# Mixer GEMMs run class by class beside attention of the other class, with buffers that live for the whole kernel

## The chip, the cores and the metric

The kernel runs on one core of a Trainium2 chip. The metric is the device time of one execution in microseconds (us); the kernel before takes 1502.11 us (median of 3 runs, 1501.19 to 1504.04).

PE is the matmul engine (PEld its weight load), DVE the vector engine, ACT the scalar engine, POOL the GpSimd engine, SP the engine that issues DMAs. PSUM is the memory that PE writes to. Each engine has its own queue of instructions, whose order is fixed when the program is built; each keeps to that order, even where a later instruction is ready.

## The reference, cut to what matters

```python
# S = 2048 tokens, D = 1024, 32 heads of 32, window W = 8 with dilation 2, F = 3584
def A(x):                       # sliding local attention
    q, k, v = split_heads(x @ wqkv)
    # token s looks at tokens s, s-2, ..., s-14: all of its own parity
    logits = einsum("bhsd,bhswd->bhsw", q, k[window(s)]) * DH ** -0.5
    o = einsum("bhsw,bhswd->bhsd", softmax(mask(logits)), v[window(s)])
    return merge_heads(o) @ wo
def B(x):                       # token-mixing MLP, contracts over ALL tokens
    h = layernorm(x)
    u = gelu(einsum("bsd,sf->bdf", h, w1) + b1)          # GEMM1
    return (einsum("bdf,fs->bds", u, w2) + b2).transpose # GEMM2
x = A_x
for layer in (1, 2):
    x = x + A(layernorm(x))
    x = x + B(layernorm(x))
```

Attention never mixes even and odd tokens, because the dilation is 2. The kernels call each parity a *class* and work on one class, split into 4 groups of 8 heads, at a time: 8 *chunks* in a layer. GEMM1 sums over all tokens, so it can be split by class into two partial sums. GEMM2 gives each token's output by itself, so it can be split by class too.

## The kernel before

Scores and weighted sums are elementwise work on DVE. Q, k, v and the output projection are matmuls.

```python
def qk(ci):                                        # scores of one chunk
    for w in range(W):
        pr = t4p.tile([P, J, QW], BF16, tag="t4")  # 3 buffers
        mult(pr, q_sb, k_window(w))                # 128x2048
        add(pr, halves of pr)                      # 128x1024
        add(St[:, w], quarters of pr)              # 128x512
    ...                                            # softmax
def pv(ci):                                        # weighted sum of v
    if c == 0: ... 8 x (DVE multiply, 4 matmuls with the identity add up in PSUM)
    else:      ... 8 DVE multiplies, 7 DVE adds
# ... after the chunks, for the first class:
for j in range(J):                                 # out-projection + residual; statistics on ACT
    ...
    nc.scalar.activation(out=junk2, in_=xn, func=ACT.Square, bias=nm[:, j], accum_out=ss[:, j])
nc.gpsimd.tensor_scalar(out=sc, in0=ss, scalar1=(1.0 + EPS) / D, scalar2=EPS * EPS, ...)   # L331
nc.gpsimd.tensor_tensor(out=sc, in0=sc, in1=mhalf, op=ALU.pow)
nc.gpsimd.tensor_tensor(out=bi, in0=nm, in1=sc, op=ALU.mult)                               # L334
for j in range(J):
    nc.scalar.activation(out=h2[0][..j..], in_=xq, func=ACT.Identity, bias=bi[:, j], scale=sc[:, j])
# GEMM1 partial sums of the first class (5 of 7 blocks of F), then layer_B:
# the rest of GEMM1, then GEMM2 for all tokens, then layernorm and transposes for the next layer
```

The layers run one after the other: attention, GEMM1, all of GEMM2, attention again. In the trace the first class's out-projection (L301, 228 to 301 us) and part of its GEMM1 partial sums already run beside the second class's chunks, although the program text has them after the chunks.

Of the kernel before, what the change touches and what calls it, by code (L numbers as in the profile page):

```python
# [1 line left out]

# [11 lines left out]
P = 128  # L14
# [9 lines left out]

@with_exitstack
def kernel(
# [11 lines left out]
):  # L38
    nc = tc.nc
# [11 lines left out]
    NT = S // P  # L51
    JH = J // 2
    assert D == H * DH and R == 16 and J == 8 and W - 1 <= J and QW == 256 and D % 512 == 0 and KD == 2 * NQ
    NDC = D // 512
    FB = 512
    NFB = F // FB
    SBW = 256
    scale = float(DH) ** -0.5
    NPART = 5
    GF = FB // P  # L60

    const = ctx.enter_context(tc.tile_pool(name="const", bufs=1))
    stat = ctx.enter_context(tc.tile_pool(name="stat", bufs=4))
    x2p = ctx.enter_context(tc.tile_pool(name="x2p", bufs=4))
    jkp = ctx.enter_context(tc.tile_pool(name="jkp", bufs=1))
    hxp = ctx.enter_context(tc.tile_pool(name="hxp", bufs=4))
    dram = ctx.enter_context(tc.tile_pool(name="dram", bufs=1, space=bass.MemoryType.DRAM))
    w1ep = ctx.enter_context(tc.tile_pool(name="w1ep", bufs=2))
    gpp = ctx.enter_context(tc.tile_pool(name="gpp", bufs=1))
    psmm = ctx.enter_context(tc.tile_pool(name="psmm", bufs=2, space=bass.MemoryType.PSUM))  # L70
    pstp = ctx.enter_context(tc.tile_pool(name="pstp", bufs=2, space=bass.MemoryType.PSUM))
    psop = ctx.enter_context(tc.tile_pool(name="psop", bufs=2, space=bass.MemoryType.PSUM))
    psgp = ctx.enter_context(tc.tile_pool(name="psgp", bufs=2, space=bass.MemoryType.PSUM))
    rr = [0]

    def ps_any():
        rr[0] += 1
        pool, tag = ((psmm, "ps"), (psop, "pso"), (psgp, "psg"))[rr[0] % 3]
        return pool.tile([P, 512], FP32, name=tag, tag=tag)

    def x2(name):
        return x2p.tile([P, D], BF16, name=name, tag="x2")
# [3 lines left out]

    ident = const.tile([P, P], BF16, name="ident")
    make_identity(nc, ident[:])
    maskq = const.tile([P, W, J, HQ], FP32, name="maskq")
    nc.vector.memset(maskq[:], 0.0)  # L90
    for w in range(1, W):
        nc.vector.memset(maskq[0:1, w, 0:w, :], NEG)
    mhalf = const.tile([P, R], FP32, name="mhalf")
    nc.vector.memset(mhalf[:], -0.5)
    b1_bf = const.tile([P, FT], BF16, name="b1_bf")
    b2_bf = const.tile([P, NT], BF16, name="b2_bf")
    with nc.allow_non_contiguous_dma(reason="tiny bias loads"):
        nc.sync.dma_start(out=b1_bf[:], in_=B_b1.rearrange("(t p) -> p t", p=P))
        nc.sync.dma_start(out=b2_bf[:], in_=B_b2.rearrange("(t p) -> p t", p=P))
    b1_sb = const.tile([P, FT], FP32, name="b1_sb")  # L100
    b2_sb = const.tile([P, NT], FP32, name="b2_sb")
    nc.vector.tensor_copy(out=b1_sb[:], in_=b1_bf[:])
    nc.vector.tensor_copy(out=b2_sb[:], in_=b2_bf[:])

    xs_a1 = dram.tile([S, D], BF16, name="xs_a1")
    xs_b1 = dram.tile([S, D], BF16, name="xs_b1")
    xs_a2 = dram.tile([S, D], BF16, name="xs_a2")

    def halo_view(t2d):
        return t2d.rearrange("(p r) d -> p r d", r=R)  # L110

    def ln_single_dve(x_ap, out_ap):
        nch = D // 512
        st = stat.tile([P, nch, 6], FP32, name="ln_st", tag="ln_st")
        for c in range(nch):
            nc.vector.bn_stats(out=st[:, c, :], in_=x_ap[:, c * 512:(c + 1) * 512])
        mv = stat.tile([P, 2], FP32, name="ln_mv", tag="ln_mv")
        nc.vector.bn_aggr(out=mv[:], in_=st[:])
        ve = stat.tile([P, 1], FP32, name="ln_ve", tag="ln_ve")
        nc.gpsimd.tensor_scalar(out=ve[:], in0=mv[:, 1:2], scalar1=EPS, scalar2=None, op0=ALU.add)  # L120
        rstd = stat.tile([P, 1], FP32, name="ln_rstd", tag="ln_rstd")
        nc.gpsimd.tensor_tensor(out=rstd[:], in0=ve[:], in1=mhalf[:, 0:1], op=ALU.pow)
        nb = stat.tile([P, 1], FP32, name="ln_nb", tag="ln_nb")
        nc.gpsimd.tensor_tensor(out=nb[:], in0=mv[:, 0:1], in1=rstd[:], op=ALU.mult)
        nc.gpsimd.tensor_scalar(out=nb[:], in0=nb[:], scalar1=-1.0, scalar2=None, op0=ALU.mult)  # L125
        nc.scalar.activation(out=out_ap, in_=x_ap, func=ACT.Identity, bias=nb[:], scale=rstd[:])  # L126

    def transposes(h_ap, tp):
        for kt in range(KD):
            nc.tensor.transpose(tp[:, kt, :], h_ap[:, kt * P:(kt + 1) * P], ident[:])  # L130

    def new_hT():
        return [[hx(f"hT{c}{jh}", [P, KD, JH, P]) for jh in range(2)] for c in range(DIL)]

    def layer_A(li, hT, res_src, xs_dst, prologue=None):
        res_v = halo_view(res_src)
        dst_v = halo_view(xs_dst)
        wq_v = A_wqkv.rearrange("(kt p) c -> p kt c", p=P)
        wo_v = A_wo.rearrange("(qi hl b a) n -> qi b a hl n", qi=NQ, hl=HQ, b=2, a=16)
        h2 = [[None, None], [None, None]]  # L140
        A = ExitStack()
        wqp = A.enter_context(tc.tile_pool(name=f"wqp{li}", bufs=3))
        qp = A.enter_context(tc.tile_pool(name=f"qp{li}", bufs=2))
        kvp = A.enter_context(tc.tile_pool(name=f"kvp{li}", bufs=1))
        stp = A.enter_context(tc.tile_pool(name=f"stp{li}", bufs=1))
        t4p = A.enter_context(tc.tile_pool(name=f"t4p{li}", bufs=3))
        oqp = A.enter_context(tc.tile_pool(name=f"oqp{li}", bufs=1))
        otp = A.enter_context(tc.tile_pool(name=f"otp{li}", bufs=5))
        wop = A.enter_context(tc.tile_pool(name=f"wop{li}", bufs=1))
        smp = A.enter_context(tc.tile_pool(name=f"smp{li}", bufs=1))  # L150
        if prologue is not None:
            hT = prologue()
        oT_all = [[None] * NQ for c in range(DIL)]
        chunks = [(c, qi) for c in range(DIL) for qi in range(NQ)]
        st8 = {}

        def proj(ci, parts_):
            c, qi = chunks[ci]
            d = st8.setdefault(ci, {})
            for part in parts_:  # L160
                wt = wqp.tile([P, KD, QW], BF16, name=f"w{part}", tag="wq")
                nc.sync.dma_start(out=wt[:], in_=wq_v[:, :, part * D + qi * QW: part * D + (qi + 1) * QW])
                if part == 0:
                    buf = qp.tile([P, J, QW], BF16, name="q_sb", tag="q_sb")
                    d["q"] = buf
                else:
                    buf = kvp.tile([P, NSLOT, QW], BF16, name="k_sb" if part == 1 else "v_sb", tag="k_sb" if part == 1 else "v_sb")
                    d["k" if part == 1 else "v"] = buf
                    nc.gpsimd.memset(buf[0:1, 0:W - 1, :], 0.0)  # L169
                for jp in range(J // 2):  # L170
                    ps = psmm.tile([P, 2, QW], FP32, name="ps", tag="ps")
                    for jj in range(2):
                        j = 2 * jp + jj
                        for kt in range(KD):
                            nc.tensor.matmul(ps[:, jj, :], lhsT=hT[c][j // JH][:, kt, j % JH, :], rhs=wt[:, kt, :],  # L175
                                             start=(kt == 0), stop=(kt == KD - 1))
                    if part == 0:
                        dst = buf[:, 2 * jp:2 * jp + 2, :]
                    else:
                        dst = buf[:, W - 1 + 2 * jp:W + 1 + 2 * jp, :]  # L180
                    nc.scalar.activation(out=dst.rearrange("p j (d h) -> p j d h", h=HQ),  # L181
                                         in_=ps[:].rearrange("p j (h d) -> p j d h", d=DH), func=ACT.Identity)
                if part > 0:
                    nc.sync.dma_start(out=buf[1:113, 0:W - 1, :], in_=buf[0:112, W:NSLOT, :])
                    nc.sync.dma_start(out=buf[113:128, 0:W - 1, :], in_=buf[112:127, W:NSLOT, :])

        def qk(ci):
            q_sb, k_sb = st8[ci]["q"], st8[ci]["k"]
            St = stp.tile([P, W, J, DH // 4, HQ], BF16, name="St", tag="St")
            for w in range(W):  # L190
# [30 lines left out]

        def pv(ci):
            c, qi = chunks[ci]
            v_sb, Pb = st8[ci]["v"], st8[ci]["P"]
            o_q = oqp.tile([P, J, QW], BF16, name="o_q", tag="o_q")
            ov = o_q[:].rearrange("p j (d h) -> p j d h", h=HQ)
            on_pe = (c == 0)
# [280 lines left out]
```

## Time and profile before

| stretch, us | what | PE busy | DVE busy |
|---|---|---|---|
| 0 to 54 | prologue (layernorm of x, first projections) | 25.5 | 29.6 |
| 54 to 388 | attention, layer 1 | 276.2 | 292.5 |
| 388 to 775.5 | out-projection of the second class, GEMM1, GEMM2 | 380.9 | 109.9 |
| 775.5 to 1128 | attention, layer 2 | 294.5 | 293.1 |
| 1128 to 1502.5 | out-projection, GEMM1, GEMM2 | 370.6 | 72.0 |

Two answers of the profile stand behind it. First, the page of the kernel before: busy time and share of the span, then the span in 40 slices, where a digit is the busy share in tenths (PEclk: the granted matmul clock in tenths).

```profile
PE 1347.7 (90%) x7968; PEld 764.5 (51%) x7968; DVE 797.1 (53%) x1155; ACT 432.6 (29%) x692; POOL 145.8 (10%) x180
...
PE   3599999929999999999987998997399999999998
...
DVE  5799999973703202323217999999465231011111
...
PEclk9899999969999999999998999999699999999999
```

Second, the busy table by stretches. The columns after the stretch are its length, then busy us (and instructions) of PE, PEld, DVE, ACT and POOL, the granted clock, the DMA share and GB/s.

```profile
0.00:54.00 54.00, 25.53 (x237) 21.98 (x238) 29.62 (x70) 20.27 (x21) 8.53 (x16) 0.94 0.88 248
54.00:388.00 334.00, 276.21 (x2024) 191.98 (x2022) 292.52 (x396) 127.55 (x226) 48.14 (x17) 0.93 0.30 91
388.00:568.00 180.00, 179.82 (x834) 81.39 (x833) 50.49 (x80) 61.30 (x84) 9.35 (x32) 1.00 0.36 108
568.00:775.50 207.50, 201.04 (x1024) 94.91 (x1022) 59.37 (x110) 32.02 (x48) 22.29 (x66) 0.99 0.36 106
775.50:1128.00 352.50, 294.50 (x2141) 206.60 (x2142) 293.13 (x396) 130.13 (x232) 48.49 (x19) 0.93 0.28 84
1128.00:1502.50 374.50, 370.57 (x1717) 167.67 (x1714) 71.98 (x107) 61.38 (x83) 8.98 (x31) 1.00 0.31 94
```

How to read this: in the GEMM stretches DVE has little to do and PE is full. In the attention stretches DVE is the fuller engine. Matmuls are pipelined and their ends modelled, so "PE busy" overstates work: a 128x512 matmul is shown with 379 ns but starts every 216 ns. Counted with 216 and 109 ns (128x256), PE has about 1312 us of work, so about 190 us of the span are idle PE or a low clock.

The dip is worth a closer look, as the timeline shows it (start, duration, engine, line, operation, and in brackets the idle time before and what ended it). These lines are from the POOL, ACT, PE and DVE timelines of the kernel before.

```profile
18.54 0.27 POOL L458 TENSOR_SCALAR r_197<-mvall 128x8 f32<-128x8 f32 x1 [14.22 <-DVE mvall L456]
...
305.34 24.20 POOL L331 TENSOR_SCALAR sc<-ss 128x8 f32<-128x8 f32 x1 [14.72 <-ACT junk L328]
...
331.60 4.63 ACT L339 ACTIVATE h_3236<-xq,bi,sc 128x1024 bf16<-128x1024 bf16 x4 [26.35 <-POOL bi L334]
...
332.89 4.41 PE L351 MATMUL psg<-h_3236,w1e 128*128 128x512 bf16 x8 [28.40 <-ACT h_3236 L339]
...
328.27 1.21 DVE L254 TENSOR_TENSOR o_q<-o_q,pvtmp 128x2048 bf16<-128x2048 bf16 x1
350.11 0.42 DVE L214 TENSOR_TENSOR m_3058<-L 128x256 f32<-128x256 f32 x1 [20.63 <-ACT L L208]
```

One POOL instruction on 128x8 elements takes 24.20 us; one of the same shape (an add alone, not a multiply and an add) took 0.27 us in the prologue, where DVE was idle. It ends at 329.54, when DVE ends its last operation (328.27 + 1.21 = 329.48). ACT waits for POOL, PE for ACT, and DVE for an Exp (L208) that stands in ACT's order behind the work that waits for POOL.

### The profile page before, as it was taken

The page shows a single profiled execution, that of the slowest core. Times are in us where ns is not written, and L with a number is a line of the kernel's source. Part 1 is how long each engine was busy: PE and PEld are TensorE (multiplying, and loading weights), DVE is VectorE, ACT ScalarE, POOL GpSimd, SP SyncE. Part 2 cuts the span into 40 slices and gives each one's busy share as a digit, 9 for nine tenths or more (in the row PEclk, how much of TensorE's full clock was granted, in tenths as well). Part 3 has the DMA queues.
Part 4 walks back from the last instruction along what each step waited for, and adds up shares of the span by engine and source line. Part 5 has one row for each costly group of instructions (what it writes and reads, how often), then busy time and mean ns, then how long its engine had stood idle before and what let it go on. Part 6 is the DMA issues. An engine that isn't in the chain of part 4 may idle for free.

```text
span 1502.5 us, 19132 instructions
## 1 busy us (share of the span) xinstructions
PE 1347.7 (90%) x7968; PEld 764.5 (51%) x7968; DVE 797.1 (53%) x1155; ACT 432.6 (29%) x692; POOL 145.8 (10%) x180
## 2 busy tenths in 40 slices
PE   3599999929999999999987998997399999999998
PEld 3576776604444444444456676764144444444444
DVE  5799999973703202323217999999465231011111
ACT  3323434424344321111122333355343442100000
POOL 1001000070200000000010001002502000000000
PEclk9899999969999999999998999999699999999999
DMA  8632223314392205343312322233146321034340
GB/s 231 209 93 67 85 75 110 96 59 128 105 252 73 68 28 147 92 140 92 91 43 68 91 69 81 84 99 109 35 132 200 115 73 47 1 94 137 114 126 34
DMA packets 177655, 150.04 MB, mean 100 GB/s; under 512 B 11712, under 2 KB 150976, under 8 KB 177568
## 3 DMA queue, kind: packets, MB, share of 16 engines
q1 hardware_dynamic: 177568, 148.82, 33.3%
q8 instruction: 62, 1.02, 0.3%
q14 instruction: 25, 0.20, 0.0%
HBM read 117.45 MB, written 16.78 MB: 89 GB/s over the span
## 4 chain that ended last, share of the span: by engine, by line
PE 57%; DVE 29%; POOL 4%; ACT 3%; issue 3%; DMA 3%; SPq 0%; DVEq 0%; POOLq 0%; ACTq 0%
PE pso L426 9%; PE psg L426 8%; PE ps L426 8%; DVE pr L192 8%; DVE pvtmp L232 6%; PE psg L386 6%; PE ps L386 6%; PE psg L351 5%; PE pso L386 5%; PE ps L175 5%; DVE pr L194 4%; PE pso L301 3%; POOL sc L331 3%; DVE o_q L254 3%; DVE St L195 2%
## 5 line engine op out<-in xcount | busy, mean ns | idle before, releaser
L192 DVE TENSOR_TENSOR pr<-q_sb,k_sb 128x2048 bf16<-128x2048 bf16 x128 | 153.6, 1213 | 22.4 <-ACT k_sb L181 18.1
L232 DVE TENSOR_TENSOR pvtmp<-v_sb,Pb 128x2048 bf16<-128x2048 bf16 x120 | 142.7, 1217 | 15.1 <-DMA v_sb<-v_sb 12.7
L386 PEld LDWEIGHTS <-w1o 128*128 128x128 bf16 x896 | 87.6, 98 | 105.8
L351 PEld LDWEIGHTS <-w1e 128*128 128x128 bf16 x640 | 63.1, 99 | 143.5 <-issue 72.7
L429 DVE SCALAR_TENSOR_TENSOR xo<-pso,b_sb,xs 128x512 bf16<-128x512 f32 x22 | 16.5, 751 | 160.7 <-PE pso L426 150.3
L429 DVE SCALAR_TENSOR_TENSOR xo<-ps,b_sb,xs 128x512 bf16<-128x512 f32 x21 | 15.8, 751 | 156.8 <-PE ps L426 146.0
L194 DVE TENSOR_TENSOR pr<-pr 128x1024 bf16<-128x1024 bf16 x128 | 85.7, 683 | 0.1
L181 ACT ACTIVATE k_sb<-ps 128x512 bf16<-128x512 f32 x64 | 36.7, 596 | 120.7 <-DVE pr L192 63.9
L351 PE MATMUL psg<-h_3236,w1e 128*128 128x512 bf16 x160 | 44.2, 395 | 29.4 <-ACT h_3236 L339 28.4
L351 PE MATMUL psg<-h_9265,w1e 128*128 128x512 bf16 x160 | 43.2, 388 | 29.4 <-ACT h_9265 L339 28.4
L429 DVE SCALAR_TENSOR_TENSOR xo<-psg,b_sb,xs 128x512 bf16<-128x512 f32 x21 | 15.8, 751 | 101.4 <-PE psg L426 90.9
L254 DVE TENSOR_TENSOR o_q<-o_q,pvtmp 128x2048 bf16<-128x2048 bf16 x56 | 68.1, 1215 | 0.1
L243 PE MATMUL pva<-pvtmp,ident 128*128 128x512 bf16 x256 | 63.8, 378 | 4.5 <-DVE pvtmp L232 1.2
L181 ACT ACTIVATE v_sb<-ps 128x512 bf16<-128x512 f32 x64 | 36.6, 595 | 72.5 <-DVE pvtmp L232 38.1
L181 ACT ACTIVATE q_sb<-ps 128x512 bf16<-128x512 f32 x64 | 38.2, 599 | 58.6 <-PE ps L175 58.6
L126 ACT ACTIVATE hb<-xo,ln_nb,ln_rstd 128x1024 bf16<-128x1024 bf16 x16 | 19.8, 1240 | 119.5 <-POOL ln_nb L125 119.5
L130 PE MATMUL tph<-ident,hb 128*128 128x128 bf16 x256 | 22.6, 240 | 35.0 <-ACT hb L468 28.9
L169 POOL MEMSET k_sb<- 1x1792 bf16 x16 | 25.3, 1582 | 283.1 <-DVE pr L192 258.1
L175 PEld LDWEIGHTS <-hT_4990 128*128 128x128 bf16 x384 | 40.0, 104 | 23.3 <-issue 15.8
L195 DVE TENSOR_TENSOR St<-pr 128x512 bf16<-128x512 bf16 x128 | 51.4, 415 | 0.1
L331 POOL TENSOR_SCALAR sc<-ss 128x8 f32<-128x8 f32 x2 | 48.4, 24202 | 29.4 <-ACT junk L328 29.4
L175 PEld LDWEIGHTS <-hT_145 128*128 128x128 bf16 x384 | 38.5, 101 | 20.7 <-issue 14.8
(993 smaller groups left out, 2624.5 us busy)
## 6 DMA issues: line engine op xcount, KB each, us to landing
w1e<-in_B_w_dram SPq DMA_DIRECT2D x14, 1024.0 KB, 5.4
w1o<-in_B_w_dram SPq DMA_DIRECT2D x14, 1024.0 KB, 5.4
xt<-in_A_x_dram SPq DMA_DIRECT2D x32, 256.0 KB, 3.9
k_sb<-k_sb SPq DMA_DIRECT2D x16, 392.0 KB, 4.8
v_sb<-v_sb SPq DMA_DIRECT2D x16, 392.0 KB, 4.8
xr<-in_A_x_dram SPq DMA_DIRECT2D x16, 256.0 KB, 2.8
xs_a_114<-xn SPq DMA_DIRECT2D x16, 256.0 KB, 2.0
xs<-xs_a_114 SPq DMA_DIRECT2D x16, 256.0 KB, 2.9
```

The source lines that it names most:

```text
L175: nc.tensor.matmul(ps[:, jj, :], lhsT=hT[c][j // JH][:, kt, j % JH, :], rhs=wt[:, kt, :], start=(kt == 0), stop=(kt == KD - 1))
L181: nc.scalar.activation(out=dst.rearrange("p j (d h) -> p j d h", h=HQ), in_=ps[:].rearrange("p j (h d) -> p j d h", d=DH), func=ACT.Identity)
L192: nc.vector.tensor_tensor(out=pr[:], in0=q_sb[:], in1=k_sb[:, W - 1 - w:W - 1 - w + J, :], op=ALU.mult)
L194: nc.vector.tensor_tensor(out=pv[:, :, 0:16, :], in0=pv[:, :, 0:16, :], in1=pv[:, :, 16:32, :], op=ALU.add)
L195: nc.vector.tensor_tensor(out=St[:, w], in0=pv[:, :, 0:8, :], in1=pv[:, :, 8:16, :], op=ALU.add)
L232: nc.vector.tensor_tensor(out=dst, in0=vw, in1=pw, op=ALU.mult)
L243: nc.tensor.matmul(accs[g][:], lhsT=ident[:], rhs=tf[:, g * 512:(g + 1) * 512], start=(w == 0), stop=(w == W - 1))
L254: nc.vector.tensor_tensor(out=ov, in0=ov, in1=tv, op=ALU.add)
L331: nc.gpsimd.tensor_scalar(out=sc[:], in0=ss[:], scalar1=(1.0 + EPS) / D, scalar2=EPS * EPS, op0=ALU.mult, op1=ALU.add)
L351: nc.tensor.matmul(ps[:], lhsT=w1e[:, j, fl * P:(fl + 1) * P], rhs=h2[0][j // JH][:, j % JH, dc * 512:(dc + 1) * 512], start=(j == 0), sto ...
L386: nc.tensor.matmul(ps[:], lhsT=w1b[c][:, j, fl * P:(fl + 1) * P], rhs=h2[c][j // JH][:, j % JH, dc * 512:(dc + 1) * 512], start=(k == 0), ...
L426: nc.tensor.matmul(ps[:], lhsT=w2b[ft // HF][:, ft % HF, tl * P:(tl + 1) * P], rhs=g[ft // GF][:, ft % GF, dc * 512:(dc + 1) * 512], start ...
```

## The change

The intent is to keep PE full in attention, with GEMM work of the other class.

- GEMM2 is done class by class. After layer 1, the first class's GEMM2 runs, and layer 2's attention starts on that class at once; the second class's GEMM2 is woven into it. The first class's out-projection and GEMM1 partials are woven into the second class's attention, now in an order made by hand.
- All buffers live for the whole kernel, so nothing waits for a pool to close between layers. The three work buffers of scores and sums become one, T4, of two windows. The transposes of the attention output share one PSUM bank, where they had two in turn.
- DVE operations of the scores, and of the sums made on DVE, cover two windows each (128x4096). In layer 2 no weighted sum is made on PE.
- The scale of the layernorms comes from Ln and Exp on ACT, not from POOL.
- For the first layernorm x is read once, into the space of GEMM1's output, not twice; the residual still reads it again.

The core of the diff; cuts are marked with `...`.

```diff
-    for w in range(W):
-        pr = t4p.tile([P, J, QW], BF16, name="pr", tag="t4")
-        nc.vector.tensor_tensor(out=pr[:], in0=q_sb[:], in1=k_sb[:, ...], op=ALU.mult)
-        ... add halves, add quarters into St[:, w]
+    for u0 in range(0, W, WB):                       # WB = 2, one buffer T4
+        nc.vector.tensor_tensor(out=flat, in0=qb, in1=windows(k, u0, WB, ...), op=ALU.mult)
+        ... add halves, quarters, eighths into St[:, u0:u0 + WB]
+        yield 0.0, 4.9                               # (PE us, DVE us) for the weave
...
-    nc.gpsimd.tensor_scalar(out=sc[:], in0=ss[:], ...)
-    nc.gpsimd.tensor_tensor(out=sc[:], in0=sc[:], in1=mhalf[:, 0:J], op=ALU.pow)
+    nc.scalar.activation(out=ln[:], in_=var, func=ACT.Ln, bias=eps[:], scale=mul)
+    nc.scalar.activation(out=dst, in_=ln[:], func=ACT.Exp, scale=-0.5)
...
+    for b in range(2):                               # transposes of the attention output
+        tp = pstp.tile([P, J, P], BF16, name="tpo", tag="tpa")      # one PSUM bank
+        ... 8 transposes; nc.scalar.copy(out=oT[:, b], in_=tp)
...
+    # GEMM2 of one class: every second column of w2 is the weight
+    nc.tensor.matmul(ps[:], lhsT=w2t[ft // HF][:, ft % HF, c::DIL], rhs=g[...], ...)
...
+    def weave(lead, fill, then, last):
+        for unit in chain(lead, last):
+            if unit == "second":                     # the other class must be ready: drain
+                for u in fill: add(u)
+                ...
+            if unit == "out":                        # let out-projection and partials in
+                fill, then = then or fill, None
+                ...
+            add(unit)
+            while t[0] < t[1]: add(next(fill))       # give PE as much as DVE has got
...
+    weave(at_.stream(), second_class(),
+          chain(out_proj(at_, 0, ..., on_act=True), partials()),
+          out_proj(at_, 1, ..., on_act=False))
+    ... rest of GEMM1; layer 1: GEMM2 of the first class; layer 2: GEMM2 of both
```

The function `weave` works while the program is built. Each unit of attention, and each unit of the GEMM work that is to fill its gaps (the fill), comes with the author's estimate of its PE and DVE time. `weave` adds these up in two accounts, and while PE's account is below DVE's, it issues fill.

## The prediction

> **What bounds the kernel now.** The busy table by stretches splits the 1502.5 us in two. The dense stretches, 388 to 762 and 1128 to 1502 us (out-projection of the second class, GEMM1, GEMM2), are full of matmuls: the chain of waits shows 128x512 matmuls every 0.216 us (28 in 6.04 us) and 128x256 ones every 0.109 us (32 in 3.50 us). The other 754 us are attention and what leads into it. There VectorE (DVE) leads: 204.9 us PE and 217.3 us DVE busy in the 220 us from 80 to 300; then PE is busy for 10 of 40 us (300 to 340, granted clock 0.62), in the chain behind a 24.2 us POOL instruction (pow) of the layernorm. The prologue delays dense PE work to about 80 us; 762 to 775 is a gap.
>
> PE work at those rates (an estimate): 2 x (1536 x 0.109 + 2048 x 0.216) = 1220, weighted sum of v on PE 256 x 0.216 = 55, residuals 7, transposes about 30: 1312 us. So PE idles, or waits on a low clock, some 190 us.
>
> **What the change does.**
> - Removes 128 weighted-sum matmuls (layer 2 sums on DVE): PE falls to about 1284 us; DVE gains 28 adds of 1.215 us, 34 us.
> - Removes POOL pow (2 x 24 us in the chain) for Ln and Exp on ACT.
> - Loads x once and early; first-class layernorm on DVE. First score multiply at about 38 us instead of 54, without the 32 us that the first chunk's scores took.
> - Layer 1: no second-class GEMM2 (97 us) before attention; it fills layer 2's attention. Out-projection (31 us) and GEMM1 partials (69 us) of the first class fill the second class's chunks.
> - DVE ops get twice as wide but run in dependent order on one T4 buffer: dependent ops start their duration plus 0.04 us apart, independent ones 0.08 us under it. Two windows of scores: about 4.75 us against 4.2 before plus the share of one 2048-wide add. I see little DVE gain: about 35 us per chunk with sums on PE, 43.5 with sums on DVE.
>
> **Sum (estimates from those durations).** Layer 1: scores start 38; 4x35 + 4x43.5, plus 10 us of DVE waiting for PE in the weighted sums: 362. Out-projection 28 + 5: 395. GEMM1 rest 576 x 0.216: 519. First-class GEMM2 and transposes: 620. Layer 2: layernorm latency, k and q of chunk 0: 641. Four chunks 174 + 12 of GEMM2 evictions + 5: 832. Second-class projection cannot start before its GEMM2 ends, so DVE idles about 22: 854. Four chunks + 5: 1033. Out-projection 32: 1065. GEMM1 608 x 0.216: 1196. GEMM2 193.5 + 3: about 1392.
>
> The strided weight load (every second column of w2) should stay hidden: a load takes 98 ns against 216, and the Trainium skill, "TensorE: Matmul & The Clock Gate", section on weight-path modes, allows fast weight load with column steps up to 1,024 elements. No run here shows it yet.
>
> **Predicted 1390 us**, 8 in 10 within 1345 to 1440. Faster by over 2%: 0.96; within 2%: 0.03; slower: 0.01.
>
> **What would show it.** Right: no POOL work in the chain; first score multiply near 38; dense stretches at 0.216 us; attention about 325 us in layer 1 and 395 in layer 2, DVE over 90% busy there; a DVE hole near 20 us where layer 2 changes class; 100 to 120 us of PE idle left.
>
> **What would make it wrong.** w2 loads (1.8 MB per 12 us, six buffers) stalling first-class GEMM2; weight loads above 216 ns; in-order DVE stalling on woven evictions (slower); the wide DVE ops losing or gaining rate; less idle at the joints than I charge (faster, toward 1340).

## More of the kernel before

The two dips of PE to 2 and 3 in the slices fall into the attention stretches, at about 300 and 1050 us.

## The result

The changed kernel takes 1398.7 us (median of 4 runs, 1396.64 to 1400.82), the kernel before 1502.88 us in the same rounds. The ratio is 0.9305 (95% interval 0.9289 to 0.9321). A ratio is the mean time of one kernel's fast runs over that of the other's of the same rounds, so it is not quite the ratio of the medians quoted. Run again, the changed kernel took 1399.62 us (ratio 0.9308).

> The changed kernel once more, so that the other runs of this call can be compared with it on the same chip. Both theories: 1395 to 1402 us.

The page of the changed kernel, the same lines as before:

```profile
PE 1314.1 (94%) x7840; PEld 749.7 (54%) x7840; DVE 818.0 (59%) x928; ACT 483.4 (35%) x940; POOL 10.5 (1%) x20
...
PE   6999989999899999999899989899949999999998
...
DVE  4869999999820433327999939929976023211111
...
PEclk9999999999999999999999999999969999999999
```

PE's 128 fewer instructions are the weighted sums moved to DVE in layer 2. POOL's work inside the layers is gone (10.5 us are left, in the first slice). One dip of PE is left, about slice 30 (1010 to 1050 us). DVE has dips to 3 and 2 inside layer 2's attention that were not there before. The busy table by stretches of the changed kernel, with bounds at its own events:

```profile
0.00:358.50 358.50, 323.53 (x2369) 222.58 (x2370) 311.19 (x336) 193.87 (x399) 10.49 (x20) 0.99 0.40 114
358.50:615.50 257.00, 255.88 (x1226) 117.06 (x1227) 86.02 (x140) 55.99 (x97) 0.00 (x0) 0.99 0.43 127
615.50:634.50 19.00, 18.84 (x161) 15.09 (x160) 2.85 (x5) 5.86 (x11) 0.00 (x0) 1.00 0.46 138
634.50:817.00 182.50, 173.06 (x1178) 111.24 (x1177) 174.23 (x172) 75.52 (x150) 0.00 (x0) 0.98 0.50 145
817.00:839.60 22.60, 19.52 (x168) 15.48 (x167) 0.34 (x2) 12.05 (x22) 0.00 (x0) 1.00 0.44 128
839.60:1037.00 197.40, 169.72 (x1124) 109.03 (x1123) 165.18 (x156) 91.92 (x183) 0.00 (x0) 0.94 0.34 95
1037.00:1394.90 357.90, 353.54 (x1625) 159.25 (x1623) 78.17 (x120) 48.24 (x78) 0.00 (x0) 0.99 0.34 102
```

Against the kernel before, by bounds that mark nearly the same events: layer 1's attention ends at 358.5 in place of 388 (29.5 us earlier; by the start of its last transposes, 358.5 against 382.8, it is 24). The GEMM stretch of layer 1 is 257 us in place of 387.5: half of GEMM2 (97 us) is gone from it, and 576 GEMM1 matmuls are left after the last transposes of attention in place of 727 (counted by their weight loads; 151 x 0.216 is 33 us). Layer 2, from its first projections to the end of attention (615.5 to 1037), takes 421.5 in place of 352.5 us, because that half is now in it. The last stretch is 357.9 in place of 374.5, as 608 GEMM1 matmuls are left after attention in place of 727. The sum, -29.5 - 130.5 + 69 - 16.6, is -107.6, the difference of the two profiled spans.

DVE's timeline of the changed kernel shows its two big holes in layer 2. The first operation of both attentions is here as well.

```profile
39.46 2.29 DVE L288 TENSOR_TENSOR T_126<-q_116,k_118 128x4096 bf16<-128x4096 bf16 x1 [16.24 <-DMA k_118<-k_118]
...
634.51 2.29 DVE L288 TENSOR_TENSOR T_126<-q_116,k_118 128x4096 bf16<-128x4096 bf16 x1 [14.16 <-ACT q_116 L275]
...
839.58 2.29 DVE L288 TENSOR_TENSOR T_126<-q_116,k_118 128x4096 bf16<-128x4096 bf16 x1 [22.26 <-ACT q_116 L275]
...
941.99 1.22 DVE L346 TENSOR_TENSOR o_q<-T_126 128x2048 bf16<-128x2048 bf16 x1 [23.78 <-PE tpo L357]
```

The hole of 22.26 us is the class change: the second class's projections cannot begin before its GEMM2, layernorm and transposes are done. The one of 23.78 us was not foreseen. DVE wants to write o_q, but PE has not yet transposed the previous chunk's o_q. The PE and ACT timelines say why:

```profile
892.88 1.06 PE L357 MATMUL tpo<-ident,o_q 128*128 128x128 bf16 x8
...
940.30 0.99 ACT L358 COPY oT<-tpo 128x1024 bf16<-128x1024 bf16 x1
...
941.34 0.61 PE L357 MATMUL tpo<-ident,o_q 128*128 128x128 bf16 x8
```

The first half was transposed at 892.88. Its copy out of the one PSUM bank stands in ACT's order behind the layernorm of woven out-projection tiles and runs at 940.30, 47 us later; in between ACT idles for 1.25 us several times while it waits for an out-projection tile. Only then can PE transpose the second half and release o_q. PE itself was busy meanwhile with the woven work, but then idles 17.7 us before the last transposes:

```profile
1034.35 1.03 PE L357 MATMUL tpo<-ident,o_q 128*128 128x128 bf16 x8 [17.70 <-DVE o_q L350]
```

### The profile page after: what moved, and what is told of

It reads as the page before. It is cut to its first block, busy times and chain, and to the rows that moved or that the text cites. A ratio compares the mean times of both kernels' runs of the same rounds, so it can differ in the third digit from the quotient of the medians.

```text
span 1394.9 us, 18742 instructions
## 1 busy us (share of the span) xinstructions
PE 1314.1 (94%) x7840; PEld 749.7 (54%) x7840; DVE 818.0 (59%) x928; ACT 483.4 (35%) x940; POOL 10.5 (1%) x20
## 4 chain that ended last, share of the span: by engine, by line
PE 56%; DVE 35%; ACT 6%; issue 2%; DMA 2%; SPq 0%; DVEq 0%; ACTq 0%
PE psg L488 11%; PE pso L488 9%; PE psg L466 9%; DVE T_126 L321 8%; PE ps L273 7%; DVE T_126 L288 7%; PE pso L433 6%; PE pso L466 5%; PE ps L466 4%; DVE T_126 L289 4%; DVE o_q L350 3%; DVE T_126 L349 3%; DVE T_126 L290 2%; DVE St L291 1%; DVE xo L493 1%
## 5 line engine op out<-in xcount | busy, mean ns | idle before, releaser
L433 PE MATMUL pso<-wo,oT 128*128 128x512 bf16 x512 | 121.5, 389 | 0.7 <-DVE xn L439 0.4
L288 DVE TENSOR_TENSOR T_126<-q_116,k_118 128x4096 bf16<-128x4096 bf16 x32 | 73.2, 2289 | 55.5 <-ACT q_116 L275 36.4
L433 PEld LDWEIGHTS <-oT 128*128 128x128 bf16 x512 | 50.4, 100 | 62.2 <-issue 7.5
L321 DVE TENSOR_TENSOR T_126<-v_120,Pb 128x4096 bf16<-128x4096 bf16 (+1 forms) x40 | 74.0, 1864 | 11.7 <-PE psg L336 10.8
L289 DVE TENSOR_TENSOR T_126<-T_126 128x2048 bf16<-128x2048 bf16 x64 | 78.1, 1221 | 1.2
L288 DVE TENSOR_TENSOR T_126<-q_117,k_119 128x4096 bf16<-128x4096 bf16 x32 | 73.1, 2284 | 4.1 <-PE psg L336 2.2
L321 DVE TENSOR_TENSOR T_126<-v_121,Pb 128x4096 bf16<-128x4096 bf16 (+1 forms) x40 | 73.8, 1864 | 0.9
L273 PE MATMUL ps<-wq,hT_152 128*128 128x256 bf16 x384 | 51.4, 288 | 4.7 <-DMA wq<-in_A_wqkv_dram 2.1
L273 PE MATMUL ps<-wq,hT_6303 128*128 128x256 bf16 x384 | 46.5, 280 | 4.6 <-ACT v_120 L275 4.2
L273 PE MATMUL ps<-wq,hT_4874 128*128 128x256 bf16 x384 | 46.5, 280 | 4.5 <-ACT v_120 L275 4.1
L358 ACT COPY oT<-tpo 128x1024 bf16<-128x1024 bf16 x32 | 32.3, 1010 | 47.3 <-PE tpo L357 47.3
L273 PE MATMUL ps<-wq,hT_153 128*128 128x256 bf16 x384 | 44.9, 273 | 3.1 <-ACT hT_153 L244 2.5
L273 PEld LDWEIGHTS <-hT_152 128*128 128x128 bf16 x384 | 38.9, 103 | 14.3 <-ACT hT_152 L244 2.9
L273 PE MATMUL ps<-wq,hT_810 128*128 128x256 bf16 x384 | 44.9, 273 | 1.7 <-ACT q_117 L275 1.0
L273 PE MATMUL ps<-wq,hT_811 128*128 128x256 bf16 x384 | 45.5, 273 | 0.4 <-ACT v_120 L275 0.4
L290 DVE TENSOR_TENSOR T_126<-T_126 128x1024 bf16<-128x1024 bf16 x64 | 44.0, 688 | 1.4
L350 DVE TENSOR_TENSOR o_q<-o_q,T_126 128x2048 bf16<-128x2048 bf16 x36 | 44.1, 1225 | 1.2
L349 DVE TENSOR_TENSOR T_126<-T_126 128x2048 bf16<-128x2048 bf16 x36 | 44.1, 1224 | 1.1
```

Source lines behind the costliest of these rows:

```text
L273: nc.tensor.matmul(ps[:, jj, :], lhsT=self.hT[c][j // JH][:, kt, j % JH, :], rhs=wts[part][:, kt, :], start=(kt == 0), stop=(kt == KD - 1))
L288: nc.vector.tensor_tensor(out=flat, in0=qb, in1=windows(k, u0, WB, [(1, J * QW)]), op=ALU.mult)
L289: nc.vector.tensor_tensor(out=pr[:, :, 0:16, :], in0=pr[:, :, 0:16, :], in1=pr[:, :, 16:32, :], op=ALU.add)
L290: nc.vector.tensor_tensor(out=pr[:, :, 0:8, :], in0=pr[:, :, 0:8, :], in1=pr[:, :, 8:16, :], op=ALU.add)
L321: nc.vector.tensor_tensor(out=dst.rearrange("p u j (d h) -> p u j d h", h=HQ), in0=v, in1=pw, op=ALU.mult)
L349: nc.vector.tensor_tensor(out=tf[:, 0], in0=tf[:, 0], in1=tf[:, 1], op=ALU.add)
```

## Experiments

Eleven more runs were made, in three calls; the kernel before ran in each call (1500.96, 1504.86 and 1503.83 us), and the ratios given are to it.

### 1. Is the 23.8 us stall real time, or PE's backlog seen from DVE? (e2_tpf)

```diff
-tp = pstp.tile([P, J, P], BF16, name="tpo", tag="tpa")
+tp = pstp.tile([P, J, P], BF16, name="tpo", tag="tpf" if b else "tpa")
```

> Changed kernel, but the transposes of the second half of the attention output go to the other transpose bank, so that they need not wait for ScalarE's copy of the first half. Theory (a bad place in ScalarE's order holds the copy, the one bank and the one o_q buffer, and stops DVE for 23.8 us in layer 2, while PE idles 18.7 us before the last transposes later): the 24 us DVE stall goes or shrinks below 8 us, time falls by 10 to 20 us to about 1379 to 1389. Rival (layer 2's second class is bound by PE anyway, 73.7 of 78.4 and 23.2 of 24.0 us busy around the stall): DVE just waits elsewhere, the time moves by less than 5 us.

Measured: 1378.16 us, ratio 0.9181 against 0.9305. DVE no longer waits at that write, and PE waits 2.35 us, not 17.7, before the last transposes. The DVE and PE timelines of this run:

```profile
921.62 1.23 DVE L346 TENSOR_TENSOR o_q<-T 128x2048 bf16<-128x2048 bf16 x1
...
1014.00 1.07 PE L357 MATMUL tpo<-ident,o_q 128*128 128x128 bf16 x16 [2.35 <-DVE o_q L350]
```

Attention ends 20 us earlier (1014.00 against 1034.35), and so does the kernel. The rival falls: the stall was the changed kernel's own loss, made by one bank, one buffer and a bad place in ACT's order. A second o_q buffer would have tested the other half of the cause, but did not fit into memory.

### 2. What the POOL instruction cost the kernel before (e5_before_lnexp, e5b_before_nopool)

In the kernel before, alone, the scale was moved to ACT:

```diff
-nc.gpsimd.tensor_scalar(out=sc[:], in0=ss[:], scalar1=(1.0 + EPS) / D, scalar2=EPS * EPS, ...)
-nc.gpsimd.tensor_tensor(out=sc[:], in0=sc[:], in1=mhalf[:, 0:J], op=ALU.pow)
+nc.scalar.activation(out=sc[:], in_=ss[:], func=ACT.Ln, bias=eps2[:], scale=(1.0 + EPS) / D)
+nc.scalar.activation(out=sc[:], in_=sc[:], func=ACT.Exp, scale=-0.5)
```

> Kernel before, with the two POOL instructions per layer that make the layernorm scale of the first class (one of them 24.2 us in each layer) replaced by Ln and Exp on ScalarE. Theory (POOL can't read while DVE streams two-input operations: the same form takes 0.25 us where DVE is idle; it ends only as DVE runs dry, and DVE runs dry because ScalarE waits for POOL): the waits of 20.6 us on DVE and 28.4 us on PE go in both layers, 40 to 50 us faster, about 1455. Rival (the stretch is bound by DVE's own work, which only shifts): under 10 us.

Measured: 1497.28 us, ratio 0.9979. The number is the rival's, and the theory seemed to fall. But POOL's timeline in this run shows that one POOL instruction was still in the chain, and that the wait had moved to it:

```profile
310.08 21.05 POOL L336 TENSOR_TENSOR bi<-nm,sc 128x8 f32<-128x8 f32 x1 [17.87 <-ACT sc L334]
```

This operation took 0.20 us before. So the edit had not taken away what it was meant to. The second try also moves `bi = nm * sc` to ACT, as 8 small activations:

> Kernel before, with all three POOL instructions of the first class's layernorm scale on ScalarE (in the last such run the wait only moved from the tensor_scalar to the next POOL instruction, 21.05 us, again until DVE ran dry). Theory (POOL starves under DVE's stream, and ScalarE, PE and then DVE wait for it): the waits of 20.6 us on DVE and 28.4 us on PE go in both layers, 35 to 50 us faster, about 1455. Rival (DVE's own work bounds the stretch, and the hole is only moved): under 10 us.

Measured: 1461.94 us, ratio 0.9721, 42 us faster. The first GEMM1 partial waits 6.7 us where it waited 28.4:

```profile
312.19 7.38 PE L354 MATMUL psg<-h,w1e 128*128 128x512 bf16 x14 [6.70 <-ACT h L342]
```

DVE's wait of 20.6 us on the Exp is gone too. So taking two tiny POOL chains off the path is worth 42 us in the kernel before, where the whole change gains 104, and needs an edit of a few lines (3 out, 6 in). The rival, that DVE's own work bounds the stretch, falls.

Why was POOL slow? The Trainium skill, "SBUF — State Buffer", section "Who interferes with whom", says that a DVE instruction with two SBUF inputs contends with a POOL instruction that reads SBUF, not with one that only writes, and calls the contention an exclusive lock. The trace agrees in kind: in the DVE stream POOL's memsets, which only write, kept their 1.58 us, while two reading instructions took 24.20 us (kernel before) and 21.05 us (first try). But the page speaks of a lock for one instruction; here POOL stayed out across 30 DVE instructions in a row (24.14 us of DVE busy in the 24.20), until DVE ran dry. That POOL stalled on this port is the page's mechanism and fits the trace; no run here looked at the port itself.

### 3. What the weave is worth (e4_noweave, e4c_noweave_tpf)

```diff
+if not first:
+    at_.split = False
+    run(second_class())                # the second class's GEMM2 before attention
-weave(at_.stream(), second_class(),
+weave(at_.stream(), second_class() if first else iter(()),
```

> Changed kernel, with the second class's GEMM2 of layer 1 run before layer 2's attention, not beside it. Theory (the weave saves its 97 us of PE time, but pays for it with the 22 us DVE hole at the class change, the 24 us stall and 12 us of evictions on DVE): attention of layer 2 becomes bound by DVE alone, about 350 us, and the whole is 35 to 45 us slower, about 1437. Rival (the weave's 97 us are its gain in full): about 1490. If the time hardly moves, the weave is not where the gain comes from.

Measured: 1479.03 us, ratio 0.9856, 80 us slower than the changed kernel; my figure was missed by 42 us. DVE's timeline has the reason:

```profile
1026.48 2.29 DVE L288 TENSOR_TENSOR T<-q,k 128x4096 bf16<-128x4096 bf16 x1 [48.73 <-ACT q L275]
```

The weave keeps accounts of PE and DVE time. With nothing to fill in the first class, DVE was far ahead in the accounts, so that the whole out-projection and most partials were issued in one lump as soon as they were let in, ahead of the next projections. That hole is an artefact of the edit. The second try sets the accounts to zero when "out" comes, and has the second transpose bank of experiment 1:

```diff
             if unit == "out":
                 fill, then = then or fill, None
+                t[:] = [0.0, 0.0]
```

> As the run with the second bank for the transposes (1378 us), but the second class's GEMM2 runs before layer 2's attention, and the fill's accounts are set to zero when the out-projection is let in, so that it is not all issued at once (that was the 48.7 us DVE hole of the first unwoven run, 1479 us). Theory (woven GEMM2 saves its 97 us of PE time less what attention gets longer): layer 2's attention takes about 350 us on DVE, from 739 to about 1092, then 345 more: about 1437, so the weave is worth about 60 us. Rival (the first unwoven run's 1479 shows the weave's true worth, 80 to 100 us): 1465 or more.

Measured: 1429.24 us, ratio 0.9496. The woven run to set beside it is e8a_reset of experiment 5 (1367.13 us, ratio 0.9091): it has the second bank and the reset too, and differs in the weave alone. The quotient of the ratios is 1.045, some 61 us; the medians differ by 62. (The two runs are of different calls. Against experiment 1's run, which lacks the reset, it would be 47 to 51.) The theory's 60 us hold, and the rival falls. Attention in layer 2 without the weave is bound by DVE, 97% busy in it:

```profile
738.00:1077.00 339.00, 272.99 (x1988) 194.63 (x1986) 328.80 (x312) 130.01 (x246) 0.00 (x0) 0.91 0.31 88
```

The first scores and the last transposes of layer 2's attention, first without the weave, then with it (e8a_reset):

```profile
737.90 2.29 DVE L288 TENSOR_TENSOR T<-q,k 128x4096 bf16<-128x4096 bf16 x1 [15.07 <-ACT q L275]
...
1077.00 1.89 PE L357 MATMUL tpo<-ident,o_q 128*128 128x128 bf16 x16 [5.68 <-DVE o_q L350]
```

```profile
634.94 2.29 DVE L288 TENSOR_TENSOR T<-q,k 128x4096 bf16<-128x4096 bf16 x1 [14.16 <-ACT q L275]
...
1015.13 1.07 PE L357 MATMUL tpo<-ident,o_q 128*128 128x128 bf16 x16 [0.34 <-DVE o_q L350]
```

Without the weave attention begins 103 us later and ends 62 us later, and in both runs 576 GEMM1 matmuls are left after it. So the weave takes GEMM2's 97 us (448 matmuls at 0.216) from before attention, but over a third of it is paid back: attention takes 380 us with it and 339 without. The hole at the class change (22 us) and the evictions, DVE's reads of GEMM2's results from PSUM (16 x 0.75 us), are the likely parts; they were not tested apart.

### 4. Do the two-window DVE operations gain anything? (e7_narrow_tpf, e7b_narrow)

The groups of the changed kernel on DVE, in order of time, four operations for two windows:

```profile
634.51 2.29 DVE L288 TENSOR_TENSOR T_126<-q_116,k_118 128x4096 bf16<-128x4096 bf16 x1 [14.16 <-ACT q_116 L275]
636.83 1.22 DVE L289 TENSOR_TENSOR T_126<-T_126 128x2048 bf16<-128x2048 bf16 x1
638.09 0.69 DVE L290 TENSOR_TENSOR T_126<-T_126 128x1024 bf16<-128x1024 bf16 x1
638.82 0.42 DVE L291 TENSOR_TENSOR St<-T_126 128x512 bf16<-128x512 bf16 x1
639.27 2.29 DVE L288 TENSOR_TENSOR T_126<-q_116,k_118 128x4096 bf16<-128x4096 bf16 x1
```

Each starts its predecessor's duration plus 0.03 to 0.04 us later: 4.76 us for two windows. The Trainium skill, "Perfetto Trace Analysis", section "Optimizing Scalar/DVE Operations", says that larger operations can help where an engine is saturated, and that half of the profiled data-access overhead of an instruction overlaps with the next instruction. No such overlap shows here, where each operation reads what the last one wrote. The edit makes the windows one by one, in the two halves of T4, in an order where neighbours are independent:

```diff
-nc.vector.tensor_tensor(out=flat, in0=qb, in1=windows(k, u0, WB, ...), op=ALU.mult)
-... three adds, each over both windows
+for u in range(WB):
+    nc.vector.tensor_tensor(out=T4[:, u], in0=q[:], in1=k[:, u0 + u:u0 + u + J, :], op=ALU.mult)
+for n in (16, 8):
+    for u in range(WB): ... add halves of pu[u]
+for u in range(WB): ... add into St[:, u0 + u]
```

and the sums likewise: 8 multiplies and 7 adds that alternate between the halves.

> As the run with the second bank for the transposes (1378 us), but scores and sums are made one window at a time in two interleaved, independent halves of T4, as the kernel before did. Theory (two-window operations gained nothing: dependent operations start their duration plus 0.02 us apart, independent ones 0.08 under it): two windows of scores go from 4.77 to about 4.57 us, the sums of a chunk on DVE from 18.2 to about 17.2 us; layer 1's attention, bound by DVE, ends 8 to 12 us earlier, in layer 2 less; 1364 to 1372. Rival (fewer, wider instructions are what keeps DVE fast): 5 to 20 us slower.

Measured: 1401.13 us, ratio 0.9318, 23 us slower than experiment 1. By the number the rival wins. But layer 1's attention did end some 10 us earlier, and from 930 to 1014 us PE was busy 58.67 us, where the run of experiment 1 had 75.41. After attention 760 GEMM1 matmuls were left, not 640; 120 x 0.216 is 26 us. The cause was mine: the edit told the weave 13.8 us for a chunk's sums, where DVE takes about 17, so that less fill was issued. With that estimate mended (four yields of 4.5 us, not three of 4.6):

> The narrow-operation run again (1401 us), with its sums' time stated rightly to the weave: there I told it 13.8 us per chunk where DVE takes 17, so that it wove in less fill and left 760 GEMM1 matmuls behind attention in place of 640. Theory (that miscount, not the narrow operations, cost the time; layer 1's attention did end 10 us earlier): 640 again, 1362 to 1370 us. Rival (narrow operations cost something I do not see): 1380 or more.

Measured: 1363.52 us, ratio 0.9064 against 0.9181. DVE's timeline:

```profile
191.87 2.36 DVE L290 TENSOR_TENSOR T<-q,k 128x2048 bf16<-128x2048 bf16 x2
194.15 1.96 DVE L293 TENSOR_TENSOR T<-T 128x1024 bf16<-128x1024 bf16 x4
196.03 0.49 DVE L295 TENSOR_TENSOR St<-T 128x256 bf16<-128x256 bf16 x2
196.43 2.35 DVE L290 TENSOR_TENSOR T<-q,k 128x2048 bf16<-128x2048 bf16 x2
```

The same work takes 4.56 us (191.87 to 196.43), as twice as many instructions. So the wide operations of the change, in the dependent order in which it wrote them, cost time rather than saved it: 15 us by the medians, 18 by the ratios. The edit changes width and order together. That the order costs, and not the width, is read from the spacings; a run with wide, independent operations would need a second T4 and was not made.

### 5. Is the fill let in too late at the class change? (e8a_reset, e8b_narrow_reset)

The reset of the accounts alone, on experiment 1's kernel, then with experiment 4's operations.

> The run with the second transpose bank (1378 us), and the weave's accounts set to zero when the out-projection is let in. Theory (at the class change in layer 2 the accounts count 21 us of projection as PE's lead, though DVE waits for it, so fill comes late; 64 GEMM1 matmuls, 14 us, are left behind attention, while PE has about 9 us idle in it): none left behind, 1366 to 1374 us. Rival (PE has no room there, so the attention gets longer by what is woven in): 1376 to 1380.

Measured: 1367.13 us, ratio 0.9091 against 0.9181. Attention ends as before (last transposes 1015.13 against 1014.00), and 576 GEMM1 matmuls are left after it, not 640. The 21 us that PE needs for the second class's first projections had been counted as a lead, though DVE was waiting for them.

> Both: narrow, independent DVE operations with the right accounts, and the reset. Theory (layer 1 is bound by DVE and gains 10 us, layer 2 by PE and gains 5 to 10): 1352 to 1364 us. Rival (they gain the same idle time twice): about 1366.

Measured: 1356.98 us, ratio 0.9020 (0.9003 to 0.9036). The two add up for the most part. This version is correct and beats both kernels: about 42 us under the changed one, with 18 lines put in for 15.

### 6. Sums on PE at the ends of attention (e3_pe7, e9_pe_67)

```diff
-at_ = Attn(hT, (0, 1, 2, 3) if first else (), first)
+at_ = Attn(hT, (0, 1, 2, 3, 7) if first else (), first)       # e3_pe7, on the changed kernel
+at_ = Attn(hT, (0, 1, 2, 3) if first else (6, 7), first)      # e9_pe_67, on experiment 1's
```

> Changed kernel, with the weighted sum of the last chunk of layer 1 on PE. Theory (the end of layer 1's attention is bound by DVE: PE idles about 27 us there): DVE sums 18.2 us become about 9.7, attention of layer 1 ends 8 us earlier, some 4 us of GEMM1 partials are pushed behind it, time falls by about 4 us. Rival (PE work is what counts, as PE is busy 94% of the span): 32 more matmuls, 7 us, make it up to 7 us slower.

Measured: 1400.74 us, ratio 0.9335, against 0.9305 and 0.9308 for the changed kernel: no gain. The expected 8 us did not come: the last transposes of layer 1's attention start at 361.93, where they started at 361.42. The sums' matmuls began at 348.12, later than DVE was ready, since 67 woven matmuls stand ahead of them in PE's order. PE's idle time was real, but not where this edit could reach it.

> As the run with the second bank for the transposes (1378 us), but layer 2 sums its last two chunks on PE, as the kernel before did with half of its chunks. Theory (with the woven GEMM2, layer 2 is bound by PE): DVE falls by 17 us, PE rises by 14, and attention cannot end earlier than the PE work allows: 5 to 15 us slower. Rival (layer 2's attention is bound by DVE): 10 to 17 us faster.

Measured: 1402.02 us, ratio 0.9324 against 0.9181, 24 us slower; the direction is right, the size missed by 9 us or more. Attention ended about 4 us earlier, but 776 GEMM1 matmuls were left after it, not 640 (136 x 0.216 = 29 us). Two causes are mixed here, and this run does not part them: PE has 64 more matmuls, and the weave was told of less DVE time and gave out less fill. Sums of four layer-2 chunks on PE, which would be nearer to the kernel before, could not be run: a deadlock (the sums hold all four fill banks of PSUM, by the code the likely reason).

## Why the prediction was right

The time was 1398.7 us, the prediction 1390 us. Point by point:

- **First scores at 38 us:** 39.46. **Layer 1's attention ends at 362:** 358.5. **GEMM1's rest starts at 395:** 388.8. **First-class GEMM2 ends at 620:** 615.5. These stages were sums of durations read from the trace of before, and each holds within 7 us.
- **DVE's two-window operations, 4.75 us, "little DVE gain":** 4.76. Experiment 4 shows the gain is negative, as the spacing of dependent operations said. DVE waited 10.8 us for PE in the weighted sums; I had said 10.
- **"A DVE hole near 20 us where layer 2 changes class":** 22.26.
- **Strided weight load:** hidden, as the Trainium skill, "TensorE: Matmul & The Clock Gate", section on weight-path modes, let me expect from the allowed column step. With a step of 2 a load took 98 ns, exactly as long as the contiguous one before. The lines of w2's weight loads, changed kernel first (duration min/median/max in ns):

```profile
L488 PEld LDWEIGHTS <-w_10609 x28: 98/98/98, 1197.4 to 1216.8; 128*128 128x128 bf16 x28
```

```profile
L426 PEld LDWEIGHTS <-w2b_4993 x56: 98/98/98, 567.5 to 588.9; 128*128 128x128 bf16 x56
```

- **Removed POOL work:** the wait was in the chain, as I said, but I called the 24.2 us instruction a pow. It is the multiply-add ahead of the pow; the pow took 1.67 us. I also took 24.2 us for its own cost. It is a wait under DVE's stream, and experiment 2 shows what removing it is worth in the kernel before: 42 us, against the 2 x 24 us that I named.
- **Two errors in layer 2 that cancel.** The first class's half was put at 191 us and took 182.5; with a start 6.5 us earlier, the class change came 15 us before my figure. In the second half, "Four chunks + 5" (179 us) took 197.4, since it holds the 23.78 us stall on o_q. I had named "in-order DVE stalling on woven evictions" as a risk; the stall was of that kind, but on transposes whose PSUM copy stood late in ACT's order. The second is the step of the sum that failed: it has no term for the stall. Without it the kernel takes 1378 us (experiment 1), 12 us under my figure; had only the first half taken what I said, it would have been about 1414 (an estimate, 1398.7 + 15). So the range would have held either way, but that the total came within 9 us is luck.
- **"DVE over 90% busy there":** true in layer 1 (295 of 319 us) and the first class of layer 2 (95%), false in its second class (84%).
- **Idle PE, 100 to 120 us:** by the same count of work (1284 us), 111 us.

Where the 104 us came from: about 42 are POOL's (experiment 2, measured on the kernel before) and about 61 the woven GEMM2 (experiment 3, measured where the stall and the late fill are mended). The stall takes 20 back (experiment 1), the late fill 11 (experiment 5) and the wide dependent operations 15 to 18 (experiment 4). The parts overlap, so the sum is only a guide; it leaves some 47 to 50 us that no run tested apart.

The traces place most of this rest in layer 1. The POOL edit alone (e5b_before_nopool) brings the kernel before to the last transposes of layer 1's attention at 361.1 us, and the changed kernel is there at 358.5, although its first scores come 16 us earlier (39.46 against 55.44): its attention takes 13 us longer on DVE, of which experiment 4 gets some 10 back. But 734 GEMM1 matmuls are then left in the one and 576 in the other, 158 x 0.216 = 34 us. So GEMM2 starts 33 us earlier (the kernel before with the POOL edit, then the changed kernel):

```profile
546.28 4.05 PE L429 MATMUL ps<-gp,w2b 128*128 128x512 bf16 x18
```

```profile
513.13 0.59 PE L488 MATMUL pso<-g_132,w_4875 128*128 128x512 bf16 x2
```

What lets these partial sums into attention was not tested. Candidates are the earlier start and the order made by hand (the first class's out-projection starts at 198 us, in e5b_before_nopool at 229). Two more candidates for the rest lie in layer 2: 128 fewer matmuls on PE (28 us), and no gap at 762 to 775.

## What to carry to other kernels

When two engines are woven by hand, each instruction that frees a shared buffer (here a PSUM copy behind two transposes) must be followed through every in-order queue it stands in; a busy table can look full while such a place costs 20 us. A small POOL instruction that reads memory took 24 us here beside a DVE stream; such a one is better kept off the path, and when it is moved, the whole chain has to go, or the wait just moves to the next link (experiment 2). Before DVE operations are widened, look at the spacing of dependent ones in the trace, and when an edit changes the length of woven work, change the weave's estimate with it.

## What the Trainium skill lacked or had wrong

- "SBUF — State Buffer", section "Who interferes with whom", describes the lock on the shared port as one instruction long. It does not say that a reading POOL instruction can stay blocked through many back-to-back two-input DVE instructions: 24.20 us through 30 of them, against 0.27 us with DVE idle.
- "TensorE: Matmul & The Clock Gate", section "Back-to-back issue gap", gives about 131 ns per matmul as the sustained rate of weight-load and matmul pairs at N = 512, and says that the 216 ns formula over-counts there. In every GEMM stretch here such pairs start 0.216 us apart (28 in 6.04 us), so for them the formula holds and the 131 does not.
- "Perfetto Trace Analysis", section "Optimizing Scalar/DVE Operations", advises larger operations where an engine is saturated. It does not weigh this against dependence: operations that read the last one's result started their duration plus 0.03 us apart, independent ones about 0.08 us under their duration (128x2048: 1.22 us long, 1.14 us apart), and twice as many narrow, independent operations were faster (4.56 against 4.76 us).
- "TensorE: Matmul & The Clock Gate", section "Weight-path perf modes", gives the allowed column steps but no duration for a strided load: at step 2 it is 98 ns, the same as at step 1.
